# Global queries' probabilities transposed by TensorE, and multiplied by the value tiles of the local part

## The chip, the cores and the metric

The kernel runs on one core of one Trainium2 chip. The time is that of the device for one execution, in microseconds. Before the change the median of three runs is 626.93 us (623.6 to 627.05).

## What is computed

Eight batches of attention with eight heads, then a gated feed-forward with a convolution along the sequence. Every head has 512 local queries and 32 global queries of 64 numbers. A global query looks at all 544 keys; a local query looks at the 32 global keys and at the local keys within 32 places of its own.

```python
k_all = np.concatenate([k_g, k_l], axis=2)
v_all = np.concatenate([v_g, v_l], axis=2)
s_g = scale * np.matmul(q_g, k_all.transpose(0, 1, 3, 2))
out_g = np.matmul(sm(s_g), v_all)
...
out_l = np.matmul(a_l, np.concatenate([v_g, v_l], axis=2))
x = np.concatenate([out_g, out_l], axis=2)      # then (B, 544, 512)
h = np.maximum(x @ w_in, 0.0)
conv_out = ...                                   # three taps along the sequence
out = h * sigmoid(conv_out) @ w_out
```

The products of the feed-forward are made of three products of split numbers each (high by high, high by low, low by high).

## The kernel before

**Local attention.** Two heads at a time go through one chain. `LQ` loads their queries and keys (`qk`, 704 KB), `LV` their values (`vf`, 448 KB). `SC` (line 283) makes scores with 32 small matmuls, `MA` (line 313, VectorE) adds the mask and finds the least, `EX` (line 323, ScalarE) takes the exponential, `NP` (line 337) divides by the sum, `DT` (line 344, VectorE) transposes in 32x32 squares, `PV` (line 354) multiplies by the values with 56 matmuls, and `XH` and `XL` (lines 368 and 373) write the result in a high and a low part. In `vf` a partition holds one of four stretches of keys; its seven slots (`ROW`) hold the previous, own and following blocks of 32 values, and the global ones.

**Global queries.** Once a batch `G` (line 304) makes the scores of all eight heads in 16 matmuls, as two groups of four heads: the 128 partitions of a group are 4 heads by 32 queries, its 544 columns the keys. `GM`, `GE` and `GN` (lines 380 to 398) make probabilities `pg` of them. `GD` (line 403, VectorE) transposes `pg` in 32x32 squares into 17 blocks of keys, and `GP` (line 411) multiplies: 17 blocks x 4 heads x 2 groups = 136 matmuls that contract 32 keys each, one after another. Their values come from a tile of its own, `vg`, that `LW` (line 261) loads once a batch, 1088 KB. `GX` (lines 419 and 420, VectorE) writes the results beside those of the local part.

**Feed-forward.** `Z` (line 437) is a block of 12 matmuls of 128x128 by 274 columns, sixteen a batch; a chain on ScalarE, GpSimd and VectorE (lines 446 to 486) makes the gated numbers; `O` (line 500) is a block of 12 matmuls into the output, sixteen a batch. In the opening `WS` (lines 210 to 212) prepares the weights.

**Order.** A planner, `arranged`, places all these steps on five engines by a position for each kind of step (`POS` for batches 1 to 7, `POS0` for batch 0 and the weights), by estimated durations and by the number of free buffers (`SLOTS`). The program is then emitted in that order, every engine in one fixed sequence. Matrix products of attention go to `four`, half of PSUM, which is given out in two halves of two banks: a step that takes one (`pa`) waits until the step that had it has been read out.

Of the kernel before, what the change touches and what calls it, by code (L numbers as in the profile page):

```python
# [18 lines left out]
P = 128  # L19
# [28 lines left out]
NG = NB + 1  # L48
# [7 lines left out]
def attn_moe(ctx: ExitStack, tc: tile.TileContext, qk_d, vw_d, qg_d, vg_d, w_in_d, w_out_d, cw_d, out_d):  # L56
# [24 lines left out]
    for c in range(4):  # L81
        rows = slice(c * SG, (c + 1) * SG)
        for k, sign in enumerate((1, -1)):
            nc.gpsimd.affine_select(
                out=corner[rows, k], in_=corner[rows, k], pattern=[[sign, SG]], compare_op=ALU.is_ge, fill=NEG,
                base=0, channel_multiplier=-sign,
            )
    mask = const.tile([P, NR, 4, SG], F32, name="mask")
# [147 lines left out]
    vg = {}  # L236
# [51 lines left out]
    def G(n):  # L288

        first = n - 7  # L290
        g = [groups.setdefault(2 * (n // H) + j, {}) for j in range(2)]
        for j in range(2):
            g[j]["s0"], g[j]["s1"] = four[:, j, :], four[:, 2 + j, 0:SG]
        for name in ("s0", "s1"):
            for c in range(4):
                k = heads[first + 2 * c]["qk"][:, SL:]
                for j in range(2):
                    rows = slice(j * D, (j + 1) * D)
                    if name == "s0":
                        kj = k[rows].rearrange("p (c x) -> p c x", c=4)[:, :, SG:]  # L300
                        kj = kj.rearrange("p c (h y) -> p c h y", h=2)[:, :, :, 0 : 2 * SG]
                    else:
                        kj = k[rows, 3 * SG : 4 * SG]
                    nc.tensor.matmul(  # L304
                        g[j][name][c * SG : (c + 1) * SG], lhsT=qg[n // H][rows, c, :], rhs=kj, start=True, stop=True
                    )
# [68 lines left out]
    def GM(n):  # L375
        gr = groups[n // 4]
        pg = gr["pg"] = att.tile([P, S], F32, name="pg", bufs=SLOTS["pg"])
# [8 lines left out]
    def GE(n):  # L386
        gr = groups[n // 4]
        gr["r"] = small.tile([P, 1], F32, name="gsum", bufs=SLOTS["pg"])
        nc.scalar.activation(
            out=gr["pg"], in_=gr["pg"], func=AF.Exp, scale=-1.0, bias=gr["m"][:, 0:1], accum_out=gr["r"]  # L390
        )

    def GN(n):
# [4 lines left out]
        nc.vector.tensor_scalar(out=gr["pg"], in0=gr["pg"], scalar1=sums, scalar2=None, op0=ALU.mult)  # L398

    def GD(n):  # L400
        gr = groups[n // 4]
        gr["pt"] = att.tile([P, NG, SG], F32, name="pgt", bufs=SLOTS["pgt"])
        nc.vector.transpose(out=gr["pt"].rearrange("p a q -> p (a q)"), in_=gr["pg"])

    def GP(n):
        b = n // H
        for k in range(NG):
            for c in range(4):
                rows = slice(c * SG, (c + 1) * SG)
                for j in range(2):  # L410
# [5 lines left out]
    def GX(n):  # L416
        for ct in range(NCT):
            xh, xl = x_of(n // H, ct)
            cp("GX", xh[:, 0:SG], four[:, ct, 0:SG])
            nc.vector.tensor_tensor(out=xl[:, 0:SG], in0=four[:, ct, 0:SG], in1=f(xh)[:, 0:SG], op=ALU.subtract)  # L420
# [88 lines left out]
    def ST(o):  # L509
# [5 lines left out]
        LQ=LQ, LV=LV, LG=LG, LW=LW, G=G, S=SC, M=MA, E=EX, NS=NS, NP=NP, DT=DT, P=PV, XH=XH, XL=XL,  # L515
        GM=GM, GE=GE, GN=GN, GD=GD, GP=GP, GX=GX,
# [7 lines left out]
    ps=4, pa=2, x=6, hb=2, qk=5, vf=3, vg=1, qg=2, p=4, pt=4, r=3, pg=2, pgt=2, t=2, o=2, wt=2, g0=2, g1=2,  # L524
# [12 lines left out]
    LQ=58.05, LG=-25.14, LW=56.28, LV=15.23, S=43.34, M=24.6, E=19.42, NS=12.52, NP=-5.48, DT=53.7, P=-27.99,  # L537
    XH=-175.6, XL=44.21, G=67.14, GM=95.31, GE=32.85, GN=280.08, GD=83.91, GP=-4.76, GX=38.67, PZ=6.05, RE=17.4,
    C1=-28.01, Ca=44.26, Cb=-31.8, TH=-7.09, GG=67.4, GH=63.89, GL=91.06, Oa=96.14, Ob=33.41, OE=-1.79,
    ST=-120.79, WD=-4.94, WA=16.42, WC=13.07, WH=-6.37, WL=-38.01, WS=48.47, WX=59.34,  # L540
)
POS0 = dict(
    LQ=30.12, LG=20.96, LW=87.08, LV=42.48, S=-65.43, M=54.85, E=3.93, NS=-15.59, NP=-54.14, DT=50.63, P=-34.2,
    XH=-195.16, XL=-39.43, G=7.35, GM=59.05, GE=-3.98, GN=74.09, GD=-38.4, GP=-79.07, GX=0.38, PZ=-53.17,
    RE=-27.29, C1=37.57, Ca=24.43, Cb=-35.96, TH=28.94, GG=-78.62, GH=88.48, GL=38.96, Oa=527.01, Ob=-8.83,
    OE=73.58, ST=33.32, WD=68.28, WA=3.38, WC=51.8, WH=4.63, WL=32.87, WS=19.23, WX=-33.89,
)

LATE = (123.9, 0.85)
WPOS = [8.33, 70.41, 33.43, -12.75, 8.79, 83.23, 144.54, 72.94]  # L550
# [5 lines left out]
def cost(key, e):  # L556
# [23 lines left out]
    def pe(t):  # L580
        return t, t + 175
# [15 lines left out]
    if key == "NP":  # L597
        return act(P, 4, more=93) if e == "a" else two(SL) if e == "v" else pool2(SL)
    return dict(
        LQ=dma(704), LV=dma(448), LG=dma(64), LW=dma(1088), WD=dma(1024), ST=(500, 2000),  # L600
        S=pe(890), P=pe(1050), G=pe(980), GP=pe(1800), PZ=pe(1522), Oa=pe(1508), Ob=pe(1508),
        M=(830, 910), E=(1544, 1550), NS=(400, 480), DT=(606, 690), XL=two(SL), GM=(930, 1010), GE=(733, 750),
        GN=(740, 820), GD=(640, 724), GX=(4 * 350, 4 * 350 + 80), RE=(290, 395) if e == "a" else psum(273),
# [6 lines left out]
COPIES = dict(XH=(SL, 1), GH=(2 * HALF, 0), OE=(HALF, 1), WH=(1024, 0), WX=(1024, 1))  # L610
# [5 lines left out]
MODE = dict(S=1, P=2, G=1, GP=2)  # L616
# [3 lines left out]
    p=("S", "G", "P", "GP", "PZ", "Oa", "Ob", "WS"), v=("WL", "DT"), g=(), s=("LQ", "LV", "LG", "LW", "WD", "ST"),  # L620
# [8 lines left out]
def plan(B):  # L629
# [31 lines left out]
    for n in range(N):  # L661
# [27 lines left out]
        if h == H - 1:  # L689
# [3 lines left out]
            for i in (n - 4, n):  # L693
# [164 lines left out]
def laid_out(q_l, k_l, v_l, q_g, k_g, v_g, moe_w_in, moe_conv_w, moe_w_out):  # L858
# [15 lines left out]
    va = np.concatenate([v_l.reshape(B, H, NB, SG, D), v_g.reshape(B, H, 1, SG, D)], axis=2)  # L874
    vg = c(va.reshape(B, 4, 2, NG, SG, D).transpose(0, 1, 4, 2, 3, 5)).reshape(B, P, 2, NG, D)
    qg = c(q_g.reshape(B, 4, 2, SG, D).transpose(0, 2, 4, 1, 3)).reshape(B, P, 4, SG)

    def bits(w):
# [3 lines left out]
        "qk": qk, "vw": vw, "qg": c(qg), "vg": vg,  # L882
# [28 lines left out]
```

## Time and profile before

| | |
|---|---|
| median of three runs | 626.93 us |
| profiled execution, its own time | 628.12 us |
| span of the profiled execution | 626.2 us |
| mean granted TensorE clock | 0.956 |
| busy: TensorE / its weight loads / VectorE / ScalarE / GpSimd | 570.4 / 529.3 / 435.7 / 343.3 / 100.2 us |
| moved by DMA | 66.17 MB |

Busy times are unions of the instructions' times, so overlapping matmuls count once. An f32 matmul leaves two records in the trace, one of the split feed-forward products one. "Issue" in a wait or in the chain is time in which an engine waited for nothing that the profile shows. The granted clock is a share of 2.4 GHz; its lower level is 0.50, 1.2 GHz.

### The profile page before, as it was taken

To read this page: it belongs to the slowest core of one execution; us is meant where nothing else is said; L and a number is where in the kernel's file an instruction comes from. 1 tells how busy PE (TensorE), PEld (TensorE's weight loads), DVE (VectorE), ACT (ScalarE), POOL (GpSimd) and SP (SyncE) were. 2 spreads that over 40 slices of the span, in tenths; PEclk is the share of its full clock that TensorE was granted. 3 is DMA by queue.
4 is the path that set the end of the run, shared out by engine and by line. 5 is a ranking of instruction groups with operands and counts; after the bars stand their busy time and mean duration, and the time that the engine had idled before them with its cause. 6 is when DMAs were issued, how large, how long until landed. Compare 5 with 4: busy or idle time off the path is not lost.

```text
span 626.2 us, 25775 instructions
## 1 busy us (share of the span) xinstructions
PE 570.4 (91%) x11200; PEld 529.3 (85%) x11200; DVE 435.7 (70%) x1379; ACT 343.3 (55%) x1092; POOL 100.2 (16%) x159
## 2 busy tenths in 40 slices
PE   3376999989999899978999899998999799989997
PEld 2254879878999899978999898997999799979997
DVE  3895899848966476965887478964997379526651
ACT  5644599627676266924894197832975176303230
POOL 2130133322101011111111011201120011101110
PEclk9988899979999799998999899998999799979999
DMA  8569524230532301442126210642043200000001
GB/s 343 210 224 345 201 97 134 79 104 30 166 113 89 104 20 50 163 155 82 50 59 250 92 42 19 220 137 84 11 159 109 84 12 27 22 21 19 28 19 54
DMA packets 22146, 66.17 MB, mean 106 GB/s; under 512 B 2577, under 2 KB 11793, under 8 KB 19985
## 3 DMA queue, kind: packets, MB, share of 16 engines
q1 hardware_dynamic: 22032, 64.52, 29.3%
q8 instruction: 88, 1.44, 1.0%
q14 instruction: 26, 0.20, 0.1%
HBM read 55.60 MB, written 8.91 MB: 103 GB/s over the span
## 4 chain that ended last, share of the span: by engine, by line
PE 84%; DVE 9%; issue 5%; DMA 1%; ACT 1%; POOL 0%; SPq 0%; POOLq 0%
PE ps_h L437 32%; PE ps_o L500 32%; PE four L354 7%; PE four L283 6%; PE four L411 4%; DVE pr L313 4%; PE psw L210 2%; PE four L304 1%; DVE pt L344 1%; DVE wt L112 1%; DMA qk<-qk 1%; PE psw L212 0%; DVE wt L109 0%; PE psw L211 0%; DVE xl L373 0%
## 5 line engine op out<-in xcount | busy, mean ns | idle before, releaser
L437 PE MATMUL ps_h<-xh,w_in 128*128 128x274 f32 x1024 | 231.2, 304 | 2.3 <-issue 2.3
L500 PE MATMUL ps_o<-g,w_out 128*128 128x272 f32 x1536 | 215.1, 293 | 0.8 <-issue 0.8
L500 PEld LDWEIGHTS ps_o<-g,w_out 128*128 128x128 f32 x1536 | 203.6, 192 | 1.9 <-issue 0.9
L437 PEld LDWEIGHTS ps_h<-xh,w_in 128*128 128x128 f32 x1024 | 177.0, 197 | 9.3 <-issue 5.7
L461 DVE SCALAR_TENSOR_TENSOR t<-hb,cw,t 128x272 f32<-128x272 f32 x256 | 122.6, 510 | 44.8 <-POOL t L267 43.9
L437 PE MATMUL ps_h<-xl,w_in 128*128 128x274 f32 x512 | 152.6, 298 | 0.0
L267 POOL TENSOR_SCALAR t<-hb,cw 128x272 f32<-128x272 f32 x128 | 78.0, 614 | 447.1 <-ACT hb L446 272.1
L446 ACT ACTIVATE hb<-ps_h 128x273 f32<-128x273 f32 x128 | 50.3, 393 | 129.2 <-PE ps_h L437 125.4
L323 ACT ACTIVATE pr<-pr,negm 128x128 f32<-128x128 f32 x256 | 99.2, 391 | 13.3 <-DVE negm L313 13.2
L437 PEld LDWEIGHTS ps_h<-xl,w_in 128*128 128x128 f32 x512 | 101.4, 198 | 0.2
L337 ACT ACTIVATE pr<-pr,sums 128x128 f32<-128x128 f32 x224 | 69.1, 393 | 0.7 <-DVE sums L331 0.6
L313 DVE CUSTOM_DVE_ANT_0 pr<-four,mask 128x128 f32<-128x128 f32 x256 | 56.7, 285 | 18.3 <-PE four L283 18.1
L470 ACT ACTIVATE t<-t 128x544 f32<-128x544 f32 x64 | 42.0, 657 | 39.2 <-DVE t L461 39.0
L354 PEld LDWEIGHTS four<-pt,vf 32*64 32x64 f32 x3584 | 49.2, 135 | 16.8 <-DVE negm L313 5.8
L354 PE MATMUL four<-pt,vf 32*64 32x96 f32 (+3 forms) x3584 | 53.2, 248 | 10.5 <-DVE negm L313 5.4
L283 PE MATMUL four<-qk 64*32 64x128 f32 x2048 | 40.2, 292 | 14.4 <-DVE negm L313 6.1
L475 DVE SCALAR_TENSOR_TENSOR t<-t,hb 128x544 f32<-128x544 f32 x64 | 45.6, 716 | 10.5 <-ACT t L470 10.2
L227 ACT CAST g<-t 128x544 fp32r<-128x544 f32 x64 | 40.7, 644 | 21.2 <-DVE t L475 16.2
L344 DVE STREAM_TRANSPOSE pt<-pr 128x512 f32<-128x512 f32 x64 | 44.4, 701 | 9.9 <-ACT pr L337 7.8
L227 DVE COPY o<-ps_o 128x272 f32<-128x272 f32 x64 | 28.0, 437 | 32.7 <-PE ps_o L500 32.5
L411 PE MATMUL four<-pgt,vg 32*64 32x32 f32 x2176 | 28.4, 234 | 22.4 <-issue 22.4
L323 ACT ACTIVATION_READ_ACCUMULATOR pr<-pr,negm 128x1 f32 x256 | 48.7, 190 | 0.0
(69 smaller groups left out, 401.8 us busy)
## 6 DMA issues: line engine op xcount, KB each, us to landing
qk<-qk SPq DMA_DIRECT2D x32, 704.0 KB, 5.7
vf<-vw SPq DMA_DIRECT2D x32, 448.0 KB, 4.0
vg<-vg SPq DMA_DIRECT2D x8, 1088.0 KB, 5.5
out<-o SPq DMA_DIRECT2D x64, 136.0 KB, 1.8
raw<-w_in SPq DMA_DIRECT2D x4, 1024.0 KB, 10.6
raw<-w_out SPq DMA_DIRECT2D x4, 1024.0 KB, 8.6
qgf<-qg SPq DMA_DIRECT2D x8, 64.0 KB, 1.9
cwr<-cw SPq DMA_DIRECT2D x1, 24.0 KB, 13.6
```

The source lines that it names most:

```text
L227: nc.scalar.copy(out=out, in_=in_) if choice(key) == "a" else eng(key).tensor_copy(out=out, in_=in_)
L267: nc.gpsimd.tensor_scalar(out=out, in0=in_, scalar1=by, scalar2=0.0, op0=ALU.mult, op1=ALU.add)
L283: nc.tensor.matmul(heads[n + j]["s"][c * SG : (c + 1) * SG, r, :], lhsT=qk[rows, i * SG : (i + 1) * SG], rhs=qk[rows, a : a + P], start=Tr ...
L313: nc.vector.tensor_tensor_reduce(out=pr[:, r, :], in0=st["s"][:, r, :], in1=mask[:, r].rearrange("p a c -> p (a c)"), op0=ALU.add, op1=ALU ...
L323: nc.scalar.activation(out=st["p"][:, r, :], in_=st["p"][:, r, :], func=AF.Exp, scale=-1.0, bias=st["m"][:, r : r + 1], accum_out=two["r"] ...
L337: nc.scalar.activation(out=p[:, r, :], in_=p[:, r, :], func=AF.Copy, scale=by[:, r : r + 1])
L344: nc.vector.transpose(out=st["pt"].rearrange("p a q -> p (a q)"), in_=st["p"].rearrange("p r x -> p (r x)"))
L354: nc.tensor.matmul(four[j * D : (j + 1) * D, c, r0 * SG : (r1 + 1) * SG], lhsT=heads[n]["vf"][rows, j, m, :], rhs=heads[n + j]["pt"][rows, ...
L411: nc.tensor.matmul(four[j * D : (j + 1) * D, c, 0:SG], lhsT=vg[b][rows, j, k, :], rhs=groups[2 * b + j]["pt"][rows, k, :], start=k == 0, s ...
L437: nc.tensor.matmul(ps, lhsT=w[:, ft, ct, :], rhs=x, start=i == 0, stop=i == 3 * NCT - 1)
L461: nc.vector.scalar_tensor_tensor(out=st["t"], in0=st["h"][:, k : k + HALF], scalar=cw[:, 3 * ft + k : 3 * ft + k + 1], in1=st["t"], op0=AL ...
L500: nc.tensor.matmul(ps, lhsT=w[:, mt, ft, :], rhs=g[:, ft, :], start=ft + i == 0, stop=ft == NFT - 1 and i == 2)
```

## The change

The global probabilities are transposed by TensorE: `GT` makes five full 128x128 transposes for each of the two groups, into PSUM, and `GC` (ScalarE) copies the result to SBUF. `GD` goes. With 128 keys on the partitions the product `GP` contracts 128 keys at a time against slots 0 to 3 and the global slot of the `vf` tiles that the local part has loaded already: 2 x 5 x 4 = 40 matmuls of 128 rows by 32 columns. So `vg` and its load `LW` go, and a batch's four `vf` tiles are held until the product is done (`vf` has five buffers for three). The keys of the global scores must be in the slots' order, so `G` writes 256 columns twice instead of 512 once, 24 matmuls for 16. The product lies with queries on the partitions; `GO` (VectorE) spreads it over two halves with zeros, and `GQ`, two matmuls with a placing matrix, turns it so that `GX` finds the layout that it had. `pg` is two fixed tiles whose last 96 columns are zero.

```diff
+SLOT = tuple(ROW.index(x) for x in (0, 1, 2, 3, None))
+NG = len(SLOT)
...
-    def LW(n):
-        vg[n // H] = load.tile([P, 2, NG, D], F32, name="vg", bufs=SLOTS["vg"])
-        nc.sync.dma_start(out=vg[n // H], in_=vg_d[n // H])
...
+                    if i < 2:
+                        kj = k[rows].rearrange("p (c m x) -> p m c x", c=4, m=NK)[:, SLOT[2 * i] : SLOT[2 * i] + 2]
+                        out = g[j]["s0"][c * SG : (c + 1) * SG, i * 2 * P : (i + 1) * 2 * P]
...
-    def GD(n):
+    def GT(n):
         gr = groups[n // 4]
-        gr["pt"] = att.tile([P, NG, SG], F32, name="pgt", bufs=SLOTS["pgt"])
-        nc.vector.transpose(out=gr["pt"].rearrange("p a q -> p (a q)"), in_=gr["pg"])
+        k = 2 * SIDE["GT", n]
+        gr["t"] = four[:, k : k + 2, :].rearrange("p a x -> p (a x)")[:, 0 : NG * P]
+        for s in range(NG):
+            keys = gr["pg"][:, s * P : (s + 1) * P]
+            nc.tensor.transpose(out=gr["t"][:, s * P : (s + 1) * P], in_=keys, identity=ident)
+
+    def GC(n):
+        gr = groups[n // 4]
+        gr["pt"] = att.tile([P, NG, P], F32, name="pgt", bufs=SLOTS["pgt"])
+        cp("GC", gr["pt"].rearrange("p s x -> p (s x)"), gr["t"])
...
     def GP(n):
...
+        b, k = n // H, 2 * SIDE["GP", n]
+        po, pt = gos[b] = [four[:, k, 0 : 2 * D].rearrange("p (a d) -> p a d", a=2), four[:, k + 1, 0 : 4 * SG]]
+        for a in range(2):
+            for s in range(NG):
+                for i in range(4):
+                    c, j = 2 * a + i // 2, i % 2
                     nc.tensor.matmul(
-                        four[j * D : (j + 1) * D, c, 0:SG], lhsT=vg[b][rows, j, k, :],
-                        rhs=groups[2 * b + j]["pt"][rows, k, :], start=k == 0, stop=k == NG - 1,
+                        po[i * SG : (i + 1) * SG, a, :], lhsT=groups[2 * b + j]["pt"][:, s, c * SG : (c + 1) * SG],
+                        rhs=heads[8 * b + 2 * c]["vf"][:, j, SLOT[s], :], start=s == 0, stop=s == NG - 1,
                     )
+    def GO(n):
...
+        nc.vector.tensor_tensor(
+            out=og, in0=po[:, :, None, :].to_broadcast([P, 2, 2, D]),
+            in1=whose[:, None, :, None].to_broadcast([P, 2, 2, D]), op=ALU.mult,
+        )
...
+    def GQ(n):
+        og, pt = gos[n // H]
+        for a in range(2):
+            nc.tensor.matmul(
+                pt[:, 2 * a * SG : 2 * (a + 1) * SG], lhsT=og[:, a].rearrange("p a d -> p (a d)"),
+                rhs=place.rearrange("p a x -> p (a x)"), start=True, stop=True,
+            )
...
-    ps=4, pa=2, x=6, hb=2, qk=5, vf=3, vg=1, qg=2, p=4, pt=4, r=3, pg=2, pgt=2, t=2, o=2, wt=2, g0=2, g1=2,
+    ps=4, pa=2, x=6, hb=2, qk=5, vf=5, qg=2, p=4, pt=4, r=3, pg=2, pgt=2, og=1, t=2, o=2, wt=2, g0=2, g1=2,
...
-    LQ=58.05, LG=-25.14, LW=56.28, LV=15.23, S=43.34, M=24.6, E=19.42, NS=12.52, NP=-5.48, DT=53.7, P=-27.99,
+    LQ=0.17, LG=-1.2, LV=8.05, S=-2.21, M=-18.29, E=219.57, NS=25.61, NP=295.34, DT=213.15, P=-133.05, XH=1.69,
...
-        S=pe(890), P=pe(1050), G=pe(980), GP=pe(1800), PZ=pe(1522), Oa=pe(1508), Ob=pe(1508),
+        S=pe(890), P=pe(1400), G=pe(980), GT=pe(560, 250), GP=pe(1430), GQ=pe(250), PZ=pe(1522), Oa=pe(1508), Ob=pe(1508),
```

All positions of the planner are new, so the order of the whole program moves. On TensorE the global product of the fourth batch stood, before, between blocks of line 437 (`four` is the half of PSUM of the attention products, `pgt` the transposed probabilities):

```order
L437 MATMUL ps_h<-xl,w_in_125 128x274
L437 MATMUL ps_h<-xh,w_in_126 128x274
L411 MATMUL four<-pgt,vg 64x32 x136
L437 MATMUL ps_h<-xh,w_in_125 128x274
L437 MATMUL ps_h<-xl,w_in_125 128x274
```

Now the same place reads as follows; line 475 is line 437 of before, line 291 is line 283, line 428 the product and line 446 `GQ`:

```order
L475 MATMUL ps_h<-xh,w_in_141 128x274
L475 MATMUL ps_h<-xl,w_in_141 128x274
L475 MATMUL ps_h<-xh,w_in_142 128x274
L428 MATMUL four<-vf,pgt 32x64 x40
L291 MATMUL four<-qk 32x128 x32
L446 MATMUL four<-place,og 128x64 x2
L475 MATMUL ps_h<-xh,w_in_141 128x274
L475 MATMUL ps_h<-xl,w_in_141 128x274
L475 MATMUL ps_h<-xh,w_in_142 128x274
```

So 136 matmuls have become 40; behind them comes a block of local scores, and then the two placing matmuls, which wait for VectorE. The block of `Z` behind them is the next of its kind.

The transposes of the next batch's groups stand alone behind blocks of `Z`; this is the second of two such places (the first has a block of `Z` behind it, this one a block of `O`, line 538):

```order
L475 MATMUL ps_h<-xl,w_in_141 128x274
L475 MATMUL ps_h<-xh,w_in_142 128x274
L412 MATMUL four<-ident,pg_127 128x128 x5
L538 MATMUL ps_o<-g_4156,w_out_143 128x272
L538 MATMUL ps_o<-g_4156,w_out_144 128x272
```

They have no counterpart on TensorE before; on VectorE the two rows of line 403 are gone. There `GO` (line 437 of the changed kernel) stands like this behind the last `XL` (line 379) of a batch, ahead of the masks (line 319) of the scores that TensorE makes meanwhile:

```order
L379 TENSOR_TENSOR xl<-four,xh 128x512
L240 COPY o<-ps_o 128x272
L379 TENSOR_TENSOR xl<-four,xh 128x512
L499 SCALAR_TENSOR_TENSOR t<-hb_149,cw,t 128x272
L437 TENSOR_TENSOR og<-four,whose 128x256
L499 SCALAR_TENSOR_TENSOR t<-hb_149,cw,t 128x272
L319 ISA pr,negm<-four,mask 128x128
L319 ISA negm 128x1
```

VectorE comes to its wait for the product with one operation of line 499 (461 before) ahead of it, and that one's second half and the masks queue behind it.

## Rows read from the trace of the kernel before

**Rows 1.** The page: busy us, share of span, instructions; granted clock, 40 slices

```profile
PE 570.4 (91%) x11200; PEld 529.3 (85%) x11200; DVE 435.7 (70%) x1379; ACT 343.3 (55%) x1092; POOL 100.2 (16%) x159
PEclk9988899979999799998999899998999799979999
```

**Rows 2.** The page, the chain that ended last, share of the span by engine

```profile
PE 84%; DVE 9%; issue 5%; DMA 1%; ACT 1%; POOL 0%; SPq 0%; POOLq 0%
```

**Rows 3.** From one line 411 group to the next: first and last of six

```profile
core 0: us, PE busy (x) PEld busy (x) DVE busy (x) ACT busy (x) POOL busy (x), PEclk, DMA share, GB/s
130.47:204.27 73.80, 70.65 (x1570) 66.58 (x1569) 50.52 (x181) 45.17 (x159) 10.57 (x17) 0.95 0.31 101
488.61:549.12 60.51, 56.88 (x1006) 54.51 (x1005) 41.13 (x121) 28.55 (x85) 9.20 (x15) 0.94 0.11 36
```

**Rows 4.** Waits: engine, line, releaser, total us, times, longest us

```profile
PE four L411 <- issue: 22.4, 14, 3.9
```

**Rows 5.** Timeline of TensorE, one group: start us, us, ..., records, [idle before]

```profile
277.20 1.39 PE L411 MATMUL four<-pgt,vg 32*64 32x32 f32 x117
279.56 1.54 PE L411 MATMUL four<-pgt,vg 32*64 32x32 f32 x128 [0.98 <-issue]
283.29 0.66 PE L411 MATMUL four<-pgt,vg 32*64 32x32 f32 x27 [2.18 <-issue]
```

**Rows 6.** The page, DMA queues: packets, MB, share of 16 engines

```profile
q8 instruction: 88, 1.44, 1.0%
```

**Rows 7.** Stretches of the eight groups, line 411 alone: first, last, sum

```profile
core 0: us, PE busy (x) PEld busy (x), PEclk, DMA share, GB/s
54.48:62.60 8.12, 3.54 (x272) 3.27 (x272) 0.78 0.94 378
...
549.12:553.32 4.20, 3.09 (x272) 2.93 (x272) 1.00 0.10 31
sum 50.26, PE 27.85 PEld 25.83; mean PE 3.48 PEld 3.23
```

**Rows 8.** Chain in order of time behind that group: start us, us, what

```profile
283.95 3.04 PE ps_h L437 x12
...
288.85 1.52 PE ps_h L437 x12
```

**Rows 9.** 8 us behind each group: first and last of eight

```profile
62.60:70.60 8.00, 8.00 (x86) 6.71 (x86) 6.28 (x14) 3.10 (x6) 0.90 (x2) 0.80 0.89 329
...
553.32:561.32 8.00, 6.46 (x35) 6.23 (x31) 2.27 (x11) 0.40 (x1) 0.49 (x1) 0.57 0.01 2
```

**Rows 10.** Timeline of TensorE, blocks of lines 283, 500 and 354

```profile
185.73 1.16 PE L283 MATMUL four<-qk 64*32 64x128 f32 x64
186.82 3.28 PE L500 MATMUL ps_o<-g,w_out 128*128 128x272 f32 x24
190.03 1.59 PE L354 MATMUL four<-pt,vf 32*64 32x128 f32 x112
191.54 0.65 PE L500 MATMUL ps_o<-g,w_out 128*128 128x272 f32 x3
```

**Rows 11.** Groups by line: count, busy us, mean ns; and the page's load

```profile
L461 DVE SCALAR_TENSOR_TENSOR t<-hb,cw,t 128x272 f32<-128x272 f32 x256 | 122.6, 510 | 44.8 <-POOL t L267 43.9
L403 DVE STREAM_TRANSPOSE pgt<-pg 128x544 f32<-128x544 f32 x16 | 11.6, 728 | 0.1
L420 DVE TENSOR_TENSOR xl<-four,xh 128x32 fp32r<-128x32 f32 x32 | 6.1, 192 | 1.1
L373 DVE TENSOR_TENSOR xl<-four,xh 128x512 fp32r<-128x512 f32 x32 | 21.9, 683 | 14.1 <-ACT xh L227 13.9
L227 ACT CAST xh<-four 128x512 fp32r<-128x512 f32 x32 | 18.7, 585 | 44.0 <-PE four L354 39.4 <-DVE w_in L201 4.4
vf<-vw SPq DMA_DIRECT2D x32, 448.0 KB, 4.0
```

More of the change, by code (lines that the diff above doesn't have):

```diff
@@ L55, in attn_moe @@
 @with_exitstack
[L56 removed]
+def attn_moe(ctx: ExitStack, tc: tile.TileContext, qk_d, vw_d, qg_d, w_in_d, w_out_d, cw_d, out_d):
     nc = tc.nc
@@ L87, in attn_moe @@
             )
+    place = const.tile([P, 2, SG], F32, name="place")
+    nc.gpsimd.memset(place, 0.0)
+    whose = const.tile([P, 2], F32, name="whose")
+    nc.gpsimd.memset(whose, 0.0)
+    for j in range(4):
+        rows = slice(j * SG, (j + 1) * SG)
+        nc.gpsimd.tensor_copy(out=place[rows, j // 2, :], in_=ident[rows, rows])
+        nc.gpsimd.memset(whose[rows, j % 2 : j % 2 + 1], 1.0)
+    pgs = [const.tile([P, SL + P], F32, name=f"pg{i}") for i in range(2)]
+    for t in pgs:
+        nc.gpsimd.memset(t[:, S:], 0.0)
     mask = const.tile([P, NR, 4, SG], F32, name="mask")
@@ L293, in G @@
             g[j]["s0"], g[j]["s1"] = four[:, j, :], four[:, 2 + j, 0:SG]
-        for name in ("s0", "s1"):
+        for i in range(3):
             for c in range(4):
@@ L298, in G @@
                     rows = slice(j * D, (j + 1) * D)
-                    if name == "s0":
-                        kj = k[rows].rearrange("p (c x) -> p c x", c=4)[:, :, SG:]
-                        kj = kj.rearrange("p c (h y) -> p c h y", h=2)[:, :, :, 0 : 2 * SG]
-                    else:
[L303 to L306, printed above, removed]
+                    if i < 2:
+                        kj = k[rows].rearrange("p (c m x) -> p m c x", c=4, m=NK)[:, SLOT[2 * i] : SLOT[2 * i] + 2]
+                        out = g[j]["s0"][c * SG : (c + 1) * SG, i * 2 * P : (i + 1) * 2 * P]
+                    else:
+                        kj, out = k[rows, 3 * SG : 4 * SG], g[j]["s1"][c * SG : (c + 1) * SG]
+                    nc.tensor.matmul(out, lhsT=qg[n // H][rows, c, :], rhs=kj, start=True, stop=True)
     def MA(n):
@@ L397, in GN @@
         nc.vector.reciprocal(out=sums, in_=sums)
-        nc.vector.tensor_scalar(out=gr["pg"], in0=gr["pg"], scalar1=sums, scalar2=None, op0=ALU.mult)
-    def GD(n):
+        nc.vector.tensor_scalar(out=gr["pg"][:, 0:S], in0=gr["pg"][:, 0:S], scalar1=sums, scalar2=None, op0=ALU.mult)
+    def GT(n):
         gr = groups[n // 4]
-        gr["pt"] = att.tile([P, NG, SG], F32, name="pgt", bufs=SLOTS["pgt"])
-        nc.vector.transpose(out=gr["pt"].rearrange("p a q -> p (a q)"), in_=gr["pg"])
-    def GP(n):
[L406 to L410, printed above, removed]
+        k = 2 * SIDE["GT", n]
[3 more added lines that the diff above has]
+            nc.tensor.transpose(out=gr["t"][:, s * P : (s + 1) * P], in_=keys, identity=ident)
@@ L578, in pool1, with pe @@
         return (180 + n * 107 // 100) * calls, (180 + n * 107 // 100) * calls + 30
-    def pe(t):
-        return t, t + 175
+    def pe(t, more=175):
+        return t, t + more
     def dma(kb):
```

70 lines of the change are left out of this document (38 added, 32 removed).

## Prediction

> **What bounds the kernel now.** First the page's list of engines: TensorE is busy 91% of the span, its weight loads 85%, and no other engine above 70% [rows 1]. Then the chain that ended last: TensorE holds 84% of it, VectorE 9%, and 5% is "issue", time in which an engine waited for nothing the profile shows [rows 2]. The stretches from one global product (line 411) to the next show the same inside a batch: TensorE 70.65 of 73.80 us busy, VectorE 50.52 [rows 3]. So what counts is TensorE's own time, and its idle time at one place: of all its waits, those at line 411 for "issue" are the largest, 22.4 us in 14 stalls [rows 4].
>
> The timeline of one such group shows how they look [rows 5]: 117 matmul records, 0.98 us of nothing, 128 records in 1.54 us, 2.18 us of nothing, the last 27. (An f32 matmul leaves two records, so 136 matmuls are 272.) From one resumption to the next are 283.29 - 279.56 = 3.73 us, for exactly 128 records. The instruction queue moved 1.44 MB in 88 transfers [rows 6]; 11,200 matmuls and as many weight loads [rows 1] are 22,400 instructions, 254.5 a transfer: about 128 records with their weight loads. I read it so: instructions come in blocks of 256, one block per about 3.7 us at best, and line 411 uses a block in 1.54 us.
>
> The price of the eight groups: their stretches sum to 50.26 us [rows 7]; the clock comes after them. In the chain the next twelve matmuls of line 437 take 3.04 us, a later twelve 1.52 [rows 8]. In the 8 us behind each group the granted clock is 0.80, 0.76, 0.65, 0.76, 0.82, 0.81, 0.78 and 0.57 [rows 9] (the first and the last of these eight stand there); at its lower level, 1.2 GHz, TensorE does half, so the loss is 8 us x (8 - 5.95) = 16.4 us. Together 66.7 us, **8.33 us a batch**.
>
> Here a rule differs. The Trainium skill (Runtime: NRT & Kernel Launch, Instruction fetch mechanics) has the same 16 KiB blocks of 256 instructions, but says that fetching is hidden behind the issue of instructions. The trace has 22.4 us that are not hidden; by the rule these would have another cause. That is a rival below.
>
> **The change, part by part** (a batch, on TensorE).
>
> *Removed:* 136 matmuls of line 411, 8.33 us with stalls and clock.
>
> *The new product:* 40 matmuls, 80 records, 128 rows by 32 columns of the array, 64 columns moved. No row shows this shape. From below: line 411's pace, 1.54 us / 128 = 12 ns a record, 0.96 us. From above: line 283 runs eight tiles of 64 by 32, 64 records in 1.09 us (185.73 to 186.82) [rows 10], 17 ns each, so 136 ns in one tile; with four tiles side by side that is 34 ns a record, 2.7 us. But line 283 moves 128 columns in each of eight tiles, the new product 64 in each of four: equal columns per tile and record, so 17 ns, 1.4 us. I take 1.4.
>
> *Ten transposes.* Nearest are full 128x128 matmuls: line 437's twelve in 1.52 us [rows 8], 127 ns each, with the same weight load and 274 columns against 128. One record each gives 1.27 us, two (as other f32 matmuls leave) 2.5. I take 1.6, nearer the lower end since half the columns move.
>
> *Two placing matmuls*, 64 columns: four records, at 12 to 127 ns 0.05 to 0.5; I take 0.3. *Eight more score matmuls* (512 columns cut in two): 16 records at 17 ns, 0.27; nothing if only the columns count.
>
> Sum: 1.4 + 1.6 + 0.3 + 0.27 = 3.57 us against 8.33: 4.76 us a batch, **38.1 us in all**.
>
> *What is charged nothing.* VectorE loses two transposes of 728 ns a batch and gains one product of 256 elements (between 192 ns for 32 columns and 683 ns for 512 [rows 11]); ScalarE gains two copies of 640 columns (585 ns for 512 [rows 11]). Neither holds the path: in [rows 3] VectorE has over 19 us free per batch. One wait is new: the placing matmuls stand in TensorE's queue behind VectorE's product, and all of TensorE's work queues behind them. In the order a score block of 32 matmuls lies between, 1.09 us, against about 0.4 for the product and a semaphore; the last VectorE work before the product is one operation of 0.51 us [rows 11] that can run under the group. So nothing; were that operation late, 0.2 a batch, 1.6 us in all, and without the cover 0.4 x 8 = 3.2. The transposes stand behind blocks of line 475 (437 of before) and need the group's normalised probabilities, which VectorE writes long before in the order but in the first batches, where a late one would cost its 0.56 us. The 1088 KB load of every batch goes, 8.7 MB with its place in SP's queue; no wait for it shows, so no gain. The value tiles are held longer, in five buffers for three: after a product three loads wait in SP's queue, with a query load and a store behind them; a load lands in 4.0 us [rows 11], while the batch's values are wanted in a cluster late in the next batch. Nothing, else about 4 us once a batch. In the opening the groups of batch 0 move behind the first blocks of line 475; that takes VectorE work (1.3 us of transposes, and the rest of the two groups) out of the time when TensorE waits, and could give up to 5 us; weights may as well be the later ones there. Between +3 and -5 us I take nothing.
>
> Span 626.2 - 38.1 = 588.1. The profiled execution took 628.12, 1.9 above its span, and 1.2 above the median of the runs, 626.93; so 588.1 + 1.9 - 1.2 = **588.8 us**, say 589.
>
> **Rivals.**
>
> *A: the clock still falls.* Behind the product come a score block and two placing matmuls, 2.8 us without a full-array matmul but these two, and transposes add two more places. If it falls once a batch, at 16.4 / 8 = 2.05 us, 16.4 of the gain are lost: 605. For it: every fall after the start lies at line 411. Against: those are groups with idle time inside, and line 354's 1.5 us between other blocks [rows 10] has none behind it. The Trainium skill (TensorE: Matmul & The Clock Gate, Part 4: PE-mode transpose) says that transposes do not count as busy for the clock: it speaks for this rival, and no row here shows a transpose.
>
> *B: instructions still come too late.* In the new order three blocks of line 360 (354 of before), with 24 matmuls of line 538 between, then 12 of line 475, then product, scores and placing: 3 x 112 + 48 + 12 + 80 + 64 + 4 = 544 records, 4.25 blocks of 128, for which the fetch needs 4.25 x 3.73 = 15.9 us; the work takes 3 x 1.51 + 2 x 3.21 + 1.52 + 1.4 + 1.09 + 0.3 = 15.3. Before, 668 records in 15.7 us needed 19.5. So nearly level, 0.6 us short where 3.8 were; what is fetched ahead covers that. Should fetches slow by a fifth, 3.8 us a batch are missing; a block ahead hides some, and I put 1.5 on the path: 12 us, 601.
>
> *C: column tiles don't run side by side.* Then a record of the product has the array alone, 127 ns as in line 437: 10.2 us for 80, 12.3 a batch against 8.33, 32 us more: 658, slower. It decides from (8.33 - 2.17) / 80 = 77 ns a record. Against: line 283 starts a record of 128 columns every 17 ns, where 128 columns alone are 59 ns by line 437's pace (127 ns for 274); so its tiles do run side by side, as tiles of half the array's rows.
>
> *D: the stalls are not instructions.* If, as by the fetch rule above, they stay wherever the product stands, the clock's fall too, only the running part changes: 272 records x 12 ns = 3.26 us for 3.57, 2.5 us more in all: 629, no change. Against: the 128 records between stalls, and the transfers' size.
>
> **Numbers.** Forecast 0.72, with its own range 576 to 598 (ends of product, transposes and placing: -0.44 -0.33 -0.25 -0.27 and +1.3 +0.9 +0.2 us a batch, hardly all at once, and the opening). A 0.12, B 0.09, C 0.05, D 0.02. The range reaches to A, 573 to 606, and leaves out C, D and the far ends of the forecast. About 1% is what a measurement of this kernel can tell: faster (forecast, A, B) 0.93, same (D) 0.02, slower (C) 0.05.
>
> **What would show it.** Line 428 in 1.2 to 2.7 us with no "issue" before it and 80 records; line 412 in 0.6 to 1.3 us per five; blocks of line 475 behind the product at 1.52 us and the clock at 1.00 there; some ten instruction transfers fewer of the 88 (162 records and their weight loads a batch); from product to product some 65 us where 69.8 stand now ((549.12 - 130.47) / 6 [rows 3]). Wrong it would be if "issue" reappears at lines 360 and 428, if line 475 still runs at 3.04, or if line 446 waits for VectorE's og.

## The result and the profile after

The changed kernel takes 582.77 us (median of 4 runs, 582.57 to 583.29); the kernel before, beside it, 626.61. The ratio is 0.931, with an interval of 0.9285 to 0.9336: 43.8 us less, where 38 were forecast. The span of the profiled execution went from 626.2 to 581.0 us, 45.2 less; the mean granted clock rose from 0.956 to 0.997.

First the page of the changed kernel: the engines, the granted clock in 40 slices, the queue that moves instructions, and the chain that ended last by engine. They answer to [rows 1], [rows 6] and [rows 2].

```profile
PE 548.5 (94%) x9904; PEld 511.8 (88%) x9904; DVE 428.9 (74%) x1371; ACT 354.2 (61%) x1108; POOL 99.3 (17%) x171
PEclk9989999999999999999999999999999999999999
q8 instruction: 77, 1.26, 0.9%
PE 81%; DVE 16%; issue 1%; DMA 1%; POOL 0%; ACT 0%; POOLq 0%; ACTq 0%
```

TensorE is still the bound, and fuller: 94% for 91%. The 7s and 8s that stood in the clock's row behind every global product are gone; one dip is left, in the opening. "Issue" has shrunk from 5% of the chain to 1%, and VectorE has grown from 9% to 16%. That share is not waiting alone: over the whole program TensorE waits for VectorE 20.5 us before and 21.5 us now, while its waits for "issue" fall from 26.2 to 0.9 us. The instruction queue made 77 transfers for 88.

Busy times by stretch, with the columns of [rows 3]: a stretch from one product (now line 428) to the next, early and last; and 8 us behind a product, as in [rows 9].

```profile
120.31:193.53 73.22, 72.41 (x1495) 68.44 (x1495) 55.56 (x207) 54.03 (x190) 11.04 (x17) 1.00 0.32 105
...
452.89:512.09 59.20, 58.33 (x932) 56.31 (x931) 38.52 (x107) 29.31 (x85) 8.33 (x16) 1.00 0.13 42
...
194.79:202.79 8.00, 6.98 (x169) 6.29 (x164) 5.80 (x38) 4.00 (x20) 0.72 (x2) 1.00 0.82 272
```

The granted clock (ahead of the last two columns) is 1.00 in all of them. From the product at 120.31 to that at 512.09 are six batches: 391.78 / 6 = 65.3 us each, where 69.8 stood. The last row has about 1 us of idle time in 8: 0.54 us is the new wait for VectorE's product og, and 0.49 us a wait of the second score block for line 456, which reads the placed result. The new wait is seen in the timeline of one batch (start us, us, engine and line, [idle before]):

```profile
120.31 1.32 PE L428 MATMUL four<-vf,pgt 128*32 128x64 f32 x80
121.57 1.16 PE L291 MATMUL four<-qk 64*32 64x128 f32 x64
122.78 0.42 DVE L437 TENSOR_TENSOR og<-four,whose 128x256 f32<-128x256 f32 x1 [1.26 <-PE four L291]
123.26 0.66 PE L446 MATMUL four<-place,og 128*128 128x64 f32 x4 [0.54 <-DVE og L437]
```

The product runs without a hole: 80 records, the score block starting 1.26 us after it. But VectorE's product og, which reads only what line 428 wrote, starts at 122.78, after the end of the score block of line 291, and the placing matmuls of line 446 wait for it. The waits of the whole program (total us, times, longest) say how often:

```profile
PE four L446 <- DVE og L437: 3.2, 6, 0.6
DVE og L437 <- PE four L291: 7.3, 6, 2.0
PE four L412 <- DVE negm L319: 1.6, 6, 0.6
PE four L291 <- issue: 0.9, 1, 0.9
```

Last, the groups of the new operations (count | busy us, mean ns of one | idle before them), and the chain's step behind the placing matmuls (start us, us, what), which answers to [rows 8]:

```profile
L412 PE MATMUL four<-ident,pg 128*128 128x128 f32 x80 | 11.8, 278 | 1.9 <-DVE negm L319 1.6 <-DVE pg L404 0.3
L428 PE MATMUL four<-vf,pgt 128*32 128x64 f32 x640 | 10.6, 220 | 0.0
L446 PE MATMUL four<-place,og 128*128 128x64 f32 x32 | 5.1, 280 | 3.2 <-DVE og L437 3.2
```

```profile
123.92 1.59 PE ps_h L475 x12
```

Line 428 has no idle time before it in any batch, the stalls of [rows 4] are gone, and the twelve matmuls of line 475 behind it take 1.59 us where their like took 3.04.

### The profile page after: what moved, and what is told of

It reads as the page before. It is cut to its first block, busy times and chain, and to the rows that moved or that the text cites. A ratio compares the mean times of both kernels' runs of the same rounds, so it can differ in the third digit from the quotient of the medians.

```text
span 581.0 us, 23177 instructions
## 1 busy us (share of the span) xinstructions
PE 548.5 (94%) x9904; PEld 511.8 (88%) x9904; DVE 428.9 (74%) x1371; ACT 354.2 (61%) x1108; POOL 99.3 (17%) x171
## 3 DMA queue, kind: packets, MB, share of 16 engines
q8 instruction: 77, 1.26, 0.9%
## 4 chain that ended last, share of the span: by engine, by line
PE 81%; DVE 16%; issue 1%; DMA 1%; POOL 0%; ACT 0%; POOLq 0%; ACTq 0%
PE ps_o L538 33%; PE ps_h L475 30%; PE four L360 7%; PE four L291 5%; DVE pr L319 4%; PE four L412 2%; DVE t L499 2%; PE four L428 2%; DVE wt L125 1%; DVE pt L350 1%; PE four L312 1%; PE psw L223 1%; PE four L446 1%; DVE wt L122 1%; DMA qk<-qk 1%
## 5 line engine op out<-in xcount | busy, mean ns | idle before, releaser
L475 PE MATMUL ps_h<-xh,w_in 128*128 128x274 f32 x1024 | 221.9, 296 | 0.0
L538 PE MATMUL ps_o<-g,w_out 128*128 128x272 f32 x1536 | 212.7, 290 | 0.0
L538 PEld LDWEIGHTS ps_o<-g,w_out 128*128 128x128 f32 x1536 | 199.8, 188 | 0.8 <-issue 0.2
L475 PEld LDWEIGHTS ps_h<-xh,w_in 128*128 128x128 f32 x1024 | 169.3, 188 | 4.8 <-issue 3.0
L499 DVE SCALAR_TENSOR_TENSOR t<-hb,cw,t 128x272 f32<-128x272 f32 x256 | 126.0, 507 | 37.3 <-POOL t L275 35.9
L475 PE MATMUL ps_h<-xl,w_in 128*128 128x274 f32 x512 | 148.3, 290 | 0.0
L275 POOL TENSOR_SCALAR t<-hb,cw 128x272 f32<-128x272 f32 x128 | 75.3, 590 | 418.1 <-ACT hb L484 332.1
L475 PEld LDWEIGHTS ps_h<-xl,w_in 128*128 128x128 f32 x512 | 97.0, 189 | 0.0
L343 ACT ACTIVATE pr<-pr,sums 128x128 f32<-128x128 f32 x224 | 70.8, 394 | 0.3 <-DVE sums L337 0.3
L508 ACT ACTIVATE t<-t 128x544 f32<-128x544 f32 x64 | 42.1, 657 | 37.8 <-DVE t L499 37.2
L350 DVE STREAM_TRANSPOSE pt<-pr 128x512 f32<-128x512 f32 x64 | 43.8, 697 | 9.6 <-PE four L360 7.3
L291 PEld LDWEIGHTS four<-qk 64*32 64x32 f32 x2048 | 31.1, 112 | 21.5 <-DVE negm L319 9.7
```

What stands on the lines that cost most here:

```text
L275: nc.gpsimd.tensor_scalar(out=out, in0=in_, scalar1=by, scalar2=0.0, op0=ALU.mult, op1=ALU.add)
L291: nc.tensor.matmul(heads[n + j]["s"][c * SG : (c + 1) * SG, r, :], lhsT=qk[rows, i * SG : (i + 1) * SG], rhs=qk[rows, a : a + P], start=Tr ...
L343: nc.scalar.activation(out=p[:, r, :], in_=p[:, r, :], func=AF.Copy, scale=by[:, r : r + 1])
L350: nc.vector.transpose(out=st["pt"].rearrange("p a q -> p (a q)"), in_=st["p"].rearrange("p r x -> p (r x)"))
L475: nc.tensor.matmul(ps, lhsT=w[:, ft, ct, :], rhs=x, start=i == 0, stop=i == 3 * NCT - 1)
L499: nc.vector.scalar_tensor_tensor(out=st["t"], in0=st["h"][:, k : k + HALF], scalar=cw[:, 3 * ft + k : 3 * ft + k + 1], in1=st["t"], op0=AL ...
```

## The experiments

Theory: before, 136 matmuls in a row used up instructions faster than they came; the stalls pulled the clock down; the change takes away most of the instructions, and with them both. Rivals: the stalls belong to the place and not to the number of matmuls (D of the prediction); the gain is the arithmetic's, or the new order's; the clock minds the kind of work and not the idle time (A). And for the new wait: it belongs to VectorE's lateness, or to what the program makes it wait for. Times are medians, with the ratio to the kernel before on the same chip.

### The number of instructions: e1_split4, e2_split2

The new product with each matmul cut into four (of 16 columns), or into two (of 32).

```diff
-        for a in range(2):
+        for a, d in ((a, d) for a in range(2) for d in range(0, D, 16)):
...
+                        po[i * SG : (i + 1) * SG, a, d : d + 16],
...
+                        rhs=heads[8 * b + 2 * c]["vf"][:, j, SLOT[s], d : d + 16], start=s == 0, stop=s == NG - 1,
```

> The changed kernel with every matmul of the product cut into four of 16 columns: 160 instead of 40, the same contraction, tiles, columns and order. Instruction theory: 320 records run in 320 x 12 ns = 3.8 us for 1.25, and the stretch of three blocks of line 360, product, scores and placing has 784 records, 6.1 blocks of 128 or 22.8 us of fetching for 17.7 us of work; so 'issue' stalls of 3 to 4 us a batch are back at the product and the clock falls behind it by about 2 us, 8 us a batch: about 645 us (625 to 660). Rival, the shape of the matmuls set stalls and clock: only the records count, no 'issue', clock 1.00, 583 + 8 x 2.6 = 604 us.

> The changed kernel with every matmul of the product cut into two of 32 columns: 80 instead of 40. Instruction theory: 160 records run in 1.9 us for 1.25; the same stretch has 624 records, 4.9 blocks, 18.2 us of fetching for 15.9 us of work, 2.3 short, of which what is fetched ahead hides most: 0 to 1.5 us of 'issue' a batch, the clock falls in some batches at most; 588 to 605 us, most likely 595. Rival, shape: 583 + 8 x 0.65 = 588 us without 'issue'.

Measured: 160 matmuls 647.4 us, ratio 1.0275 (1.0187 to 1.0363), span 645.0, mean clock 0.952; 80 matmuls 608.3, ratio 0.9654 (0.956 to 0.9748), span 604.0, clock 0.983. The page and the waits of the four-fold cut, and one of its products:

```profile
PEclk9989999969999699989999699987999899979999
```

```profile
PE four L428 <- issue: 25.9, 15, 3.0
```

```profile
281.36 1.29 PE L428 MATMUL four<-vf,pgt 128*32 128x16 f32 x130
282.94 1.32 PE L428 MATMUL four<-vf,pgt 128*32 128x16 f32 x128 [0.28 <-issue]
286.66 1.05 PE L428 MATMUL four<-vf,pgt 128*32 128x16 f32 x62 [2.41 <-issue]
```

The same numbers are multiplied in the same place, and the stalls and the clock's fall of before are back. Their beat too: from 282.94 to 286.66 are 3.72 us for 128 records, where [rows 5] had 3.73 for the same 128. The trace of the kernel before shows the transfers themselves. In the 7.5 us from 277 to 284.5, which hold the group of [rows 5], the instruction queue made three:

```profile
q8 instruction: 3, 0.05, 2.9%
```

They start at 277.33, 280.69 and 284.42 us. Of all 88 no two start less than 3.29 us apart, and in none of the fourteen traces less than 3.27. So the number of instructions decides, and rival D falls. The two-fold cut came out above the range it was given, 588 to 605; in its waits the stalls stand mostly one step further on, at the score block:

```profile
PE four L291 <- issue: 9.5, 4, 3.0
```

With 160 records in the product and the score block's 64 behind them the instructions run out four times at the score block.

### The same matmuls apart: e3_spread

The kernel before, its 136 matmuls in three lots of 48, 48 and 40, with the next two blocks of lines 437 and 500 between the lots. Only the steps that read the result (lines 419 and 420) move with the last lot.

```diff
-    def GP(n):
+    def GP(n, part=None):
         b = n // H
-        for k in range(NG):
+        for k in range(NG) if part is None else range(*((0, 6), (6, 12), (12, NG))[part]):
```

> The kernel before, with the 136 matmuls of line 411 cut into three lots of 48, 48 and 40, and the next two blocks of line 437 or 500 (or 210) put between them on TensorE; the same matmuls, tiles, loads and positions. Instruction theory: the product and its two blocks need about 283 records in 6.3 us, so nearly all stalls go and the clock stays at 1.00: 626.6 - 66.7 + 8 x 3.26 = 586 us, with some rest of stalls up to 600. Rival, shape (contracting 32 rows in 32x64 tiles is slow and lowers the clock): no stall moves, at least 615 us.

Measured: 601.4 us, ratio 0.9545 (0.9479 to 0.9611), span 598.9, clock 0.993. Its page, its waits and one product:

```profile
PEclk9988999999999999999999999999999999999999
q8 instruction: 88, 1.44, 1.1%
```

```profile
PE four L411 <- issue: 1.4, 3, 0.7
PE four L283 <- DVE negm L313: 9.8, 12, 2.4
```

```profile
198.05 1.18 PE L411 MATMUL four<-pgt,vg 32*64 32x32 f32 x96
...
200.89 1.18 PE L411 MATMUL four<-pgt,vg 32*64 32x32 f32 x96
202.00 1.78 PE L500 MATMUL ps_o<-g,w_out 128*128 128x272 f32 x12
203.71 1.04 PE L411 MATMUL four<-pgt,vg 32*64 32x32 f32 x80
```

As many matmuls, as many instruction transfers (88), no new arithmetic: and of 22.4 us of "issue" 1.4 are left, and the clock's row has its dips in the opening alone. 27.3 us of the span go by spacing alone. The time is just above the 600 us that the expectation allowed, and the 27.3 us are less than the 38.8 which the stalls (22.4) and the clock (16.4) were put at. Of the 11.5 between them 1.4 are the stalls left, and 3.7 longer waits of the scores for VectorE, 9.8 us where the kernel before has 6.1; what the other 6 are was not taken apart, and stays open. The waits of the kernel before, for this and for the sum below:

```profile
PE four L283 <- DVE negm L313: 6.1, 12, 2.4
PE ps_h L437 <- issue: 2.3, 2, 1.5
PE ps_o L500 <- issue: 0.8, 1, 0.8
```

### About half the product: e4_half

The kernel before with 9 of 17 key blocks in line 411: 72 matmuls.

```diff
-        for k in range(NG):
+        for k in range(9):
```

> The kernel before with 9 of the 17 key blocks in line 411 (72 matmuls for 136); the other 8 blocks are left out of the global queries' result. Instruction theory: the stretch then has 540 records, as in the changed kernel, so no stall and no fall of the clock: 144 records x 12 ns = 1.7 us a batch for 8.33, 626.6 - 53 = 574 us (568 to 584). Rival, stalls and clock are a price per matmul of this shape: they halve, 626.6 - 66.7 x 8 / 17 = 595 us, with 'issue' of some 10 us at line 411.

Measured: 579.2 us, ratio 0.9193 (0.9115 to 0.9271), clock 0.991. The waits:

```profile
PE four L411 <- issue: 2.8, 4, 1.7
```

Half of the matmuls are worth 49.8 us (629.0 on that chip), though 64 of them running are 128 records x 12 ns = 1.5 us a batch, 12 us in all. The rest, 37.8 us, is about what stalls (22.4, of which 2.8 are left) and clock (16.4) were put at, 36.0. Both this kernel and e3 still load `vg` and still transpose on VectorE, so neither had to go for stalls and clock to get better.

### Idle time and the clock: e8_long_wait

The changed kernel with VectorE's product made eight times, so that TensorE waits some 3 us longer a batch.

```diff
-        nc.vector.tensor_tensor(
+        for _ in range(8):
+            nc.vector.tensor_tensor(
```

> The changed kernel with VectorE's spreading product done eight times over, so that TensorE waits some 8 x 0.42 - 0.42 = 2.9 us longer for it once a batch (the values are the same). Theory that idle time makes the clock fall, not the kind of matmul: the clock falls to its lower level in most batches there; 8 x (2.9 + about 1.5) = 35 us more, 618 us (605 to 625). Rival, the clock fell because of the small matmuls of line 411: clock 1.00, 8 x 2.9 = 23 us more, 606 us.

Measured: 619.2 us, ratio 0.9857 (0.9813 to 0.9901), span 619.1, clock 0.967. The timeline of one batch, the 10.8 us from its product (at 272.21) on, the first 2.6 us behind the wait of the last batch, and the waits of the whole program:

```profile
274.67 3.63 DVE L438 TENSOR_TENSOR og<-four,whose 128x256 f32<-128x256 f32 x8 [0.78 <-PE four L291]
278.36 1.12 PE L447 MATMUL four<-place,og 128*128 128x64 f32 x4 [3.74 <-DVE og L438]
```

```profile
272.21:283.00 10.79, 7.05 (x170) 6.69 (x170) 7.24 (x34) 2.86 (x13) 0.81 (x2) 0.84 0.55 196
...
551.41:554.00 2.59, 2.59 (x11) 2.59 (x12) 1.30 (x9) 0.00 (x0) 0.00 (x0) 0.50 0.00 0
```

```profile
PE four L447 <- DVE og L438: 24.5, 7, 3.8
PE four L447 <- DVE sums L336: 2.1, 1, 2.1
```

TensorE has the same instructions as in the changed kernel. Idle times for another reason bring the lower level, 1.2 GHz, back in seven batches: 3.7 us in the six in the middle, 2.03 us in the last. In the first batch 2.08 us left the clock at 1.00, so no single length of an idle time decides here. It was idle time that pulled the clock down, not the stalls' cause. The span is 38.1 us longer than the changed kernel's. The waits at the placing matmuls are 24.5 + 2.1 = 26.6 us for 3.2, 23.4 more, and 14.7 are left for the clock.

### Transposes and the clock: e11_long_turn, e10_again

The changed kernel with every five transposes made eight times, forty in a row (e11), and the changed kernel unchanged beside it (e10).

```diff
-        for s in range(NG):
+        for s in [s for _ in range(8) for s in range(NG)]:
```

> The changed kernel with every five transposes made eight times over, 40 for 5, sixteen times; the values are the same. Measures a transpose by itself and the clock under 4 us of nothing else. Theory: transposes keep the clock up like other matmuls: 35 x 0.1 us x 16 = 56 us more, 639 us, clock 1.00 behind them. Rival, the rule that transposes do not count as busy: the clock falls within or behind each lot, transposes and the blocks behind at half speed, some 16 x 2 to 3 us more: 675 us or above.

> The changed kernel itself, unchanged, beside the others on this chip: 583 us.

Measured: 644.1 us (ratio 1.0268, 1.0207 to 1.0329; span 642.5), and 583.3 (0.9298, 0.926 to 0.9336; span 581.4). The groups and the clock of e11:

```profile
L412 PE MATMUL four<-ident,pg 128*128 128x128 f32 x640 | 73.0, 274 | 1.8 <-DVE negm L319 1.6 <-DVE pg L404 0.3
```

```profile
PEclk9989999999999999999999999999999999999999
```

560 more transposes cost 642.5 - 581.4 = 61.1 us, 0.109 us each, and the clock stays at 1.00 through all sixteen stretches of forty (the mean of the run is 0.997). Rival A had the rule of the Trainium skill (TensorE: Matmul & The Clock Gate, Part 4: PE-mode transpose) behind it, that transposes do not count as busy for the clock. No run here bears that out: through 4.3 us of nothing but f32 transposes the granted clock is 1.00, and behind them too.

### Arithmetic and order apart: e5_old_order, e6_new_order

All positions of the planner are new in the change. e5 has the new arithmetic with the positions of before (the new steps keep theirs), e6 the old arithmetic with the new ones.

```diff
-    LQ=0.17, LG=-1.2, LV=8.05, S=-2.21, M=-18.29, E=219.57, NS=25.61, NP=295.34, DT=213.15, P=-133.05, XH=1.69,
+    LQ=58.05, LG=-25.14, LW=56.28, LV=15.23, S=43.34, M=24.6, E=19.42, NS=12.52, NP=-5.48, DT=53.7, P=-27.99,
```

> The changed kernel with the position tables of before (positions of the four new kinds of step kept from the new tables). Theory that the gain is instructions and clock: it does not hang on the tables; 583 to 600 us, clock 1.00 behind the product, no large 'issue'. Rival, the new order brought the gain: 610 us or more.

> The kernel before with the position tables of after (the old transpose gets the place of the new ones, the removed load keeps its own). Theory that the gain is instructions and clock: line 411 still stalls for about 3 us a batch and the clock falls behind it; 615 to 640 us, most likely 626. Rival, the new order brought the gain: 600 us or less.

Measured: e5 602.2 us, ratio 0.9578 (0.9539 to 0.9618), span 601.2; e6 621.4, ratio 0.9892 (0.9867 to 0.9917), span 618.8. So on that chip (before: 628.0) the arithmetic alone brings 25.8 us, the order alone 6.6, and both together, at 0.931, 43: some 11 come only with both. The waits of e6 keep nearly all of what [rows 4] had:

```profile
PE four L411 <- issue: 18.6, 10, 2.7
```

In e5 the six batches from its second to its last product take what they take in the changed kernel, and 21 us are lost ahead of them. First e5, then the changed kernel, by stretch, and last the same six batches of e6:

```profile
20.00:40.00 20.00, 6.92 (x187) 5.56 (x186) 15.42 (x58) 12.17 (x40) 4.40 (x4) 1.00 0.58 233
141.40:533.81 392.41, 382.06 (x7226) 362.86 (x7225) 289.22 (x970) 251.97 (x824) 56.94 (x96) 0.98 0.25 81
```

```profile
20.00:40.00 20.00, 13.68 (x393) 9.76 (x376) 19.03 (x48) 11.52 (x35) 4.53 (x4) 0.91 0.64 234
120.31:512.09 391.78, 385.23 (x7298) 366.69 (x7297) 290.19 (x974) 251.02 (x826) 57.83 (x97) 1.00 0.25 82
```

```profile
124.33:542.93 418.60, 398.69 (x8253) 377.82 (x8252) 299.39 (x979) 240.15 (x795) 58.09 (x98) 0.96 0.28 91
```

392.41 / 6 = 65.4 us a batch for 65.3 with the new arithmetic, and 418.60 / 6 = 69.8 with the old one, as in the kernel before: the steady part's gain is the arithmetic's, whatever the positions. What the positions change lies outside these six batches. The second product comes at 141.40 in e5, at 124.33 in e6, at 130.47 in the kernel before and at 120.31 in the changed one. e5 missed its range (583 to 600) by its opening; 7.0 us of that are one wait of TensorE, for ScalarE's copy `GC`, a step that the positions of before do not know. Since its table is a mixture, which opening they would make with the new steps placed well is not shown.

### The new wait: e7_block_first, e12_spread_first, e9_shifted

In e12 VectorE's product (`GO`) is emitted ahead of the score block (`S`) that stands behind line 428, and no engine's own sequence changes: only what each step is told to wait for.

```diff
+        if open_ and key == "S":
+            held.append(j)
+            continue
+        made.append(j)
+        if key == "GO":
+            made += held
```

> The changed kernel with VectorE's product (line 437) emitted ahead of the score block behind line 428; every engine's own sequence stays as it was. Theory (a step waits for all that was emitted before it on the tile `four`, whatever its part): VectorE's product starts at the end of line 428 instead of the end of the score block, no longer waiting 7.3 us for line 291; the placing matmuls lose their 3.2 us of waiting; but now the score block, emitted behind, waits for VectorE's product, about 0.6 us in each of eight batches, some 4.5 us. So the time stays within 1%: 579 to 588, with a wait of line 291 for og in the place of that of line 446. Rival (the delay lies between VectorE and TensorE themselves, not in what was emitted first): line 446 still waits 0.5 us a batch for og, and line 291 does not wait: 583. Rival (tile parts are told apart): neither waits, 577 or less.

Measured: 583.5 us, ratio 0.93 (0.9254 to 0.9345), span 581.3. The timeline of the batch shown above, and the waits:

```profile
120.36 1.32 PE L428 MATMUL four<-vf,pgt 128*32 128x64 f32 x80
121.75 0.42 DVE L437 TENSOR_TENSOR og<-four,whose 128x256 f32<-128x256 f32 x1 [0.19 <-PE four L428]
122.23 1.16 PE L291 MATMUL four<-qk 64*32 64x128 f32 x64 [0.55 <-DVE og L437]
123.32 0.66 PE L446 MATMUL four<-place,og 128*128 128x64 f32 x4
```

```profile
PE four L291 <- DVE og L437: 4.1, 6, 0.8
```

VectorE starts 1.39 us after the product's start (121.75 for 120.36) instead of 2.47 (122.78 for 120.31), so in this batch it was not late. In four of the six batches an operation of line 499 delays it by some 0.36 us, less than the score block's 1.09. The wait has only moved: now the score block, emitted behind og, waits for og, though it writes another part of `four`. So here the dependency goes by the whole tile `four`, in the order of the program. As long as score block and product lie side by side, one waits for the other.

e7 therefore puts a block of line 475 or 538 between product and scores, and the scores behind VectorE's product. e9 does the same and has one more block ahead of the second score block and of each five transposes. The diff is that of e9; `pull` emits the next block, and e7 has the first of the two calls.

```diff
+        if key == "GP":
+            made.append(j)
+            pull(k)
...
+        if second and ops[j][2] == PE:
+            if key in ("S", "GT"):
+                pull(k)
```

> The changed kernel with one block of line 475 or 538 moved between product and scores, and the scores put behind VectorE's product in the program. In the changed kernel VectorE's product starts only when the score block ends (both write the same PSUM tile), and the placing matmuls wait about 0.6 us in six of eight batches. Theory: with the block as cover that wait goes, 6 x 0.6 = 3.6 us: 579 us (577 to 581). Rival: the score block behind it, or its readers, then wait as long: 583 us.

> The changed kernel with one block of line 475 or 538 more between the steps behind the product: product, block, scores, placing, block, block, second scores, block, transposes, block, transposes. In e7 the wait only moved to the second score block, which waits for VectorE to read out the placing result (1.6 to 2.0 us in five batches). Theory: with a block more there both waits go, 579 us, some 0.6% below the changed kernel (577 to 582). Rival, each step shifted brings its own wait and the later steps of the batch then come late: 583 us or more.

Measured: e7 589.6 us, ratio 0.9384 (0.9358 to 0.941), clock 0.991: slower than the change, against its expectation. e9 579.6, ratio 0.9246 (0.9212 to 0.928), beside 583.3 for e10 on the same chip: 3.7 us less than the changed kernel, and the fastest of all that do the whole work. The waits of e7, then of e9:

```profile
PE four L291 <- DVE xl L456: 10.0, 6, 2.0
```

```profile
PE four L291 <- DVE xl L456: 0.5, 1, 0.5
```

In e7 the wait of line 446 is gone, but the second score block now waits for VectorE to read out the placed results (line 456), 10 us in all: the whole tile again, one step later. In e9 that has a block ahead of it too. TensorE's matmuls no longer wait for og, and for line 456 once, 0.5 us, as in the changed kernel.

## Why the prediction was right, point by point

**What bounds the kernel** was read rightly. Instructions in blocks of 256, one per 3.7 us: e1 repeats the beat to 0.01 us (the transfers themselves come as close as 3.3 us), and e3 takes the stalls away without touching a matmul. The Trainium skill (Runtime: NRT & Kernel Launch, Instruction fetch mechanics) has the fetch hidden behind issue; here 22.4 us were not hidden, and the measurement decides. The clock as a consequence of idle time: e8.

**Removed, 66.7 us.** Of its parts the stalls and the clock's loss are gone from the trace. The whole of it was not measured by itself.

**The product, 1.4 us a batch taken:** 1.25 us for 80 records, 15.6 ns each, 10.0 us in all for 11.2. Tiles side by side do run so; rival C (127 ns a record) falls.

**Ten transposes, 1.6 us a batch taken:** 0.98, since five take 0.52 or 0.46 us to the next instruction: 7.9 us in all for 12.8. Each leaves one record (80 for 80), which was the lower of the two ends. The pace of line 437's blocks, 127 ns, was the right neighbour; I leaned up from it without need, and e11 has 109.

**Placing, 0.3 taken:** 0.36 to 0.47 us to the next instruction, 3.5 us in all for 2.4. **Eight more score matmuls, 0.27 taken:** the global scores take 1.09 us for 1.08, so nothing, for 2.2 in all.

**The new wait, nothing taken: this step failed,** and with it one of the prediction's signs of being wrong came: line 446 waits for og. The prediction said that the score block of 1.09 us covers og and its semaphore. It doesn't, in six of eight batches: from the start of the score block to the placing matmuls are 1.69 us four times, 2.13 once and 2.90 once (0.86 of that "issue"), 4 x 0.60 + 1.04 + 1.81 = 5.25 us over 1.09. The price "without the cover" was named, 3.2 us, and the profile's waits for og sum to just that. What I overlooked is not a duration but a dependency: in the program og is told to wait for all that was emitted before it on `four`, the score block too. e12 shows it. Also charged nothing were the transposes' waits for VectorE's masks (line 319 writes negm), which with what lies around them are 1.9 us.

**The sum.** 10.0 + 7.9 + 3.5 + 5.25 + 1.9 = 28.6 us of new work, where 8 x 3.57 = 28.6 were forecast. The equality is luck: operations 7.2 us cheaper than taken, waits 7.2 dearer. So the 38.1 stood, and the 7.1 us that the span gained beyond it lie elsewhere. By stretch: the six batches from the second product to the last gain 418.65 - 391.78 = 26.9 us, where 6 x 4.76 = 28.6 were forecast. The time to the second product shrinks by 10.2 us and that behind the last product's start by 8.2 (77.1 to 68.9), 18.4 together where two batches make 9.5. The opening was put at nothing between +3 and -5, and there the sum was furthest off: e6 shows that the new positions alone bring the second product 6.1 us forward. Stalls outside line 411, which the sum had not counted, are gone as well (2.3 us of "issue" at line 437 and 0.8 at line 500, shown under e3). How the 7.1 us divide between these was not measured.

**Product to product, "some 65":** 65.3. **"Some ten transfers fewer":** 11. **Rival A**, the clock: it doesn't fall, with idle times of 0.5 us; e8 shows that 3.7 are enough, and in one batch 2.03. **Rival B**, instructions too late: one stall of 0.9 us is left of it, and e2 shows how near it was, since 80 records more in the product bring back 9.5 us.

## What to carry to other kernels

Some hundreds of small matmuls in a row cost more than they run: count the instructions of a stretch against the pace at which the trace shows them coming, and where they don't come in time, put long matmuls between the small ones, or make fewer and larger ones. Short idle times cost themselves (here 0.5 us), longer ones the clock behind them too (here 3.7 us always, 2 us once in two); so look at the granted clock behind every stall before pricing it. And before a wait is called covered, read what the waiting instruction is told to wait for: steps that share one tile wait for one another in the order of the program, even where they touch different parts of it.

## What the runs showed of the hardware beyond that

A transpose of f32 by TensorE leaves one record where other f32 matmuls here leave two, and forty in a row run at 0.109 us each with the granted clock at 1.00. Matmuls of 32 columns of the array take 15.6 ns a record with 128 rows and 64 columns moved (80 in 1.25 us), and those of 32 rows and 64 columns of the array 11.6 ns with 32 moved (96 in 1.11 us, 198.05 to 199.16 in e3). Idle times of 0.5 us left the clock alone in every batch of the changed kernel; in e8 3.7 us brought it down in six batches of six, and of two idle times of 2.0 to 2.1 us one did. The instruction queue's transfers never started less than 3.27 us apart in fourteen traces, while a product of small matmuls uses up the 128 records of one in 1.3 to 1.5 us.
